# A planned mixer-and-MLP kernel on one core: a rank for every instruction in place of a rank for every kind, and another order of the first loads

## The chip, the cores and the metric

The kernel runs on one core of one Trainium2 chip. The time is the device time of that core in microseconds (us). A core has engines that run side by side, each strictly in its own order: PE (TensorE, matmuls; its weight loads are shown apart as PEld), DVE (VectorE), ACT (ScalarE), POOL (GpSimd), and SP (SyncE), which here only issues DMAs. The engines wait for each other through semaphores. PE writes to PSUM only, and ACT carries nearly every PSUM result back to SBUF ("evicts" it).

## The reference, cut to what matters

```python
x = A_q                                          # 2048 rows of 640, bf16
g = sigmoid((x * gate_w).sum(-1))
# branch A: a causal convolution of four taps on k, times v, then a convolution of length 2048 by FFT
k_shift = sum(k_pad[:, t:t+S] * shift_k[:, 3-t] for t in range(4))
kv = k_shift * v
y = irfft(rfft(kv, 2*S) * rfft(ssm_k, 2*S))[:S] + kv * ssm_D
a = q * y
# branch B: layer norm, w1, gelu, four column groups moved by +1, -1, +2, -2 rows, w2, residual, layer norm, w3, gelu, w4, residual
h = gelu(layernorm(x) @ w1);  x1 = x + shift_groups(h) @ w2
b = x1 + gelu(layernorm(x1) @ w3) @ w4
out = g * a + (1 - g) * b
```

## The kernel before

All data stays in one SBUF tensor ("arena"). The 2048 rows stand as 2 halves (c) of 128 partitions of 8 rows (r), so "row r" below means 2 x 128 rows of the matrix, and x comes in by pieces of some r of one c.

The program is written as a list of 924 nodes (`Prog.op`, `pe`, `dma`; class `Node`, lines 32 to 63), each with an engine, a planned cost, a tag such as `mm1` or `kv`, and what it depends on. `Prog._forward` (lines 200 to 347) then fixes the order of each engine: it keeps a planned clock of each engine and of the DMA link, and takes again and again the node that could start first; among nodes that could start at the same time the one with the higher `prio` goes first. `assign_waits` and `emit` turn the orders into instructions and semaphore waits. So a planned cost, the planned rate of the link (`RATE`) and the ranks change nothing in what is computed; they change in which order each engine does it, and each engine then keeps to that order even if the data of a later instruction is there first.

The tags, in the order of the work:

- `x`: loads of x, ten DMAs by `X_LOADS` (line 438). The pieces of row 0 go by ACT's queue, the others by SP's. `w1`, `shk`, `k`, `kh`, `v`, `w2`, `FM`, `ssm`, `D`, `gw`: the other loads on SP's queue (lines 707 to 736), all through `load` (line 692).
- `bn`, `st`, `ln`, `xn`: the first layer norm. Statistics by DVE (`bn`, lines 874 and 876; row 1 by ACT, `st`, line 666), the power -1/2 by POOL (line 854), normalized rows by DVE (`xn`, line 654).
- `xTp`, `xTe`: transposition by PE (line 913) and its eviction by ACT (line 680, as nearly all evictions).
- `mm1`, `gelu1`, `tail`: w1 (line 953), gelu, and small DMAs by POOL (line 993) that move column groups.
- `kv`, `kvb`: the four taps and v, on DVE (line 649, as all its tensor_tensor operations).
- `tap`, `ssmD`, `tT`, `tW`, `tR`: the filter `ssm_k` transposed, its first half by PE (line 809), its second by DMA.
- `seed2`, `mm2`, `x1`, `sq`: x is put into PSUM by ACT (line 1043), w2 is added by PE (line 1061), the sum is evicted with its row sums, and its squares are summed by ACT (line 666).
- `fwdh`, `Sh`, `fwdk`, `Sk`: forward transforms of filter and kv by PE (line 1164) and their evictions. `:0` and `:1` belong to the first half of the columns, `:2` and `:3` to the second.
- `bh`, `win`, `bk`, `pw`, `pwz`, `fold` (`unit`, line 1263): butterflies and pointwise products, all on DVE, for four units 0 to 3.
- `mm3`, `gelu3`, `seed4`, `mm4`, `B`: w3 (line 1115) and w4 (line 1133) with their gelu, seeds and evictions.
- `inv`, `invl`, `gy`, `fin`, `out`: inverse transforms (lines 1352 and 1327), gates and stores.
- `fill`: 96 matmuls on ones (line 744) that nobody reads; the planner puts them where PE would stand.

Slots are shared: the transforms of the second half are evicted into places that the units 0 and 1 read (`s3`, `s4`), so `fwdh:3` must wait until DVE's `pw:1` has read `s4`. PSUM is four pairs of banks, so PE can be a few jobs ahead of ACT's evictions.

Of the kernel before, what the change touches and what calls it, by code (L numbers as in the profile page):

```python
# [88 lines left out]
class Prog:  # L89
# [88 lines left out]

    PRIO = {}

    def schedule(self):
        for n in self.nodes:
            n.base = frozenset(n.deps)
        for j in self.jobs:
            own = set(j.nodes)
            j.ext = [d for v in j.nodes if not v.first for d in v.base if d not in own]
            if j.seeded:
                j.nodes[0].soft = [d for v in j.pes for d in v.base if d not in own]
        for n in self.nodes:
            for d in n.deps:  # L190
                d.users.append(n)
        for n in self.nodes:
            n.prio = self.PRIO.get(n.tag, 0.0)
        self._forward()

    RATE = 400e3
# [3 lines left out]
    def _forward(self):  # L200
# [14 lines left out]
        link = 0.0  # L215
# [5 lines left out]
        duty = carry = 0.0  # L221
        LAT = self.LAT
# [16 lines left out]
        while left:  # L239
# [42 lines left out]
            if n.array:  # L282
# [7 lines left out]
                if n.tag != "shk":  # L290
                    inside = min(cost, self.PHASE + (w + 1) * self.WINDOW - t)
                    duty += inside
                    carry += cost - inside
            free[e] = t + cost
# [7 lines left out]
            elif n.kind == "acc":  # L302
                alink = max(alink, t + 1.2) + n.bytes / 220e3
# [123 lines left out]
def _bf16_bits(a):  # L427
# [10 lines left out]
X_LOADS = ((0, 1), (1, 2), (2, 4), (4, 6), (6, 8))  # L438
# [16 lines left out]
PRIO = {  # L455
# [36 lines left out]
}  # L492
# [44 lines left out]
def bass_gated_mix__ssm_conv_h3__mixer_s_mlp__prompt_kernel(  # L537
# [168 lines left out]
    for a, b in X_LOADS:  # L706
        P.stage = a
        for c in range(2):
            load(XQ.get((a, c), "sp"), X[:, c, a:b, :], rows(A_q, c)[:, a:b, :], 163840 * (b - a), tag="x", land=1.4 if b < 3 else 2.2)
    P.stage = ""  # L710
    load("pool", V(oID, 256).bitcast(U16), cI.ap(), 65536, tag="ident", cost=0.6)
    load("sp", w1v, B_w1.rearrange("(c p) f -> p c f", p=128), 890000, tag="w1")
    load("sp", SHKROW, dram(A_shift_k, 0, [[2560, 1], [1, 2560]]), 5120, tag="shk")
    w1s, w1d = w1v.rearrange("p c (g f) -> p c g f", g=4)[:, :, :, 128:160], w1t.rearrange("p c (g f) -> p c g f", g=4)
    P.op("pool", lambda e, ps: e.tensor_copy(w1d, w1s), r=[w1s], w=[w1d], cost=1.2, tag="w1t")
# [101 lines left out]
    def add_d(h):  # L817
        t0row = TAP[0:1, h, 0, :]
        P.op("pool", lambda e, ps: e.tensor_tensor(t0row, t0row, DROW[h], ALU.add), r=[t0row, DROW[h]], w=[t0row],
             cost=2.0, tag="ssmD")  # L820
# [67 lines left out]
    def sum_group(rhos):  # L888
# [6 lines left out]
        ln_finish(VAR2, RS2, 2.3, rsl)  # L895
# [507 lines left out]
    P.PRIO = PRIO  # L1403
# [32 lines left out]
```

## Time and profile before

| what | value |
|---|---|
| median of 3 runs | 228.64 us (227.26 to 228.83) |
| profiled execution, its own time | 227.51 us |
| its span, first to last instruction | 225.7 us |
| DVE busy | 208.1 us |
| ACT busy | 174.8 us |
| PE weight loads (PEld) busy | 139.0 us |

The profiled execution's own time is 1.8 us above its span, and 1.1 us below the median. The profile's "PE busy" counts a matmul from its start to the end of its latency, so it overstates how full PE is. The chain of waits follows the work that ended last back through what released it. In the timeline, equal instructions in a row are merged: start, length, engine, line, shapes, count, and in brackets how long the engine had stood before and what ended that.

### The profile page before, as it was taken

The numbers are of one execution on the slowest core, as the hardware profiler recorded it, in microseconds if no ns is written. First come the engines' busy times: TensorE is split into PE (matmuls) and PEld (weight loads), VectorE is DVE, ScalarE is ACT, GpSimd is POOL, SyncE is SP. The second block draws the span as 40 slices with busy tenths as digits, with TensorE's granted clock in tenths as the row PEclk, the third lists the DMA queues.
The fourth block names the chain that finished last, engine by engine and source line by source line (L and its number), as shares of the span: only waits on it lengthen the run. The fifth ranks groups of instructions, "written<-read, shape, count | busy, mean of one in ns | idle before, by whom it ended". The sixth has DMA issues, their size and how long they took to land.

```text
span 225.7 us, 3992 instructions
## 1 busy us (share of the span) xinstructions
PE 217.8 (97%) x1575; PEld 139.0 (62%) x1587; DVE 208.1 (92%) x267; ACT 174.8 (77%) x292; POOL 42.6 (19%) x48
## 2 busy tenths in 40 slices
PE   6999999999999999999999999999999999999992
PEld 6695855557776664457754467754465566577771
DVE  4899999999999969999999999649999999999985
ACT  5889979879999999999785885594593465574392
POOL 1143654460004220203203200000010000332010
PEclk9999999999999999999999999999999999999999
DMA  6999997779823948061441680000077018488576
GB/s 166 392 401 402 334 348 251 151 143 243 281 96 84 310 85 341 7 116 33 87 86 30 108 130 0 3 0 0 0 132 219 0 35 200 58 174 110 126 135 215
DMA packets 36714, 34.05 MB, mean 151 GB/s; under 512 B 17508, under 2 KB 31719, under 8 KB 36568
## 3 DMA queue, kind: packets, MB, share of 16 engines
q1 hardware_dynamic: 31560, 23.97, 36.7%
q0 software_dynamic: 4848, 9.50, 19.2%
q10 hardware_dynamic: 288, 0.33, 0.5%
q8 instruction: 12, 0.20, 0.4%
q14 instruction: 6, 0.05, 0.1%
HBM read 21.47 MB, written 3.93 MB: 113 GB/s over the span
## 4 chain that ended last, share of the span: by engine, by line
PE 60%; DVE 24%; DMA 5%; issue 4%; ACT 4%; SPq 2%; DVEq 0%
PE PS L1133 23%; PE PS L1115 23%; DVE arena L649 20%; PE PS L1164 8%; PE PS L1352 6%; DMA arena<-in_A_q_dram 5%; ACT arena L680 3%; SPq L692 2%; DVE arena L874 2%; DVE arena L654 1%; PE PS L1061 1%; DVE arena L876 0%; ACT PS L1043 0%; DVE arena L1337 0%; DVEq L1406 0%
## 5 line engine op out<-in xcount | busy, mean ns | idle before, releaser
L649 DVE TENSOR_TENSOR arena<-arena 128x2560 bf16<-128x2560 bf16 (+5 forms) x175 | 185.9, 1120 | 10.4 <-ACT arena L680 8.9
L680 ACT ACTIVATE arena<-PS 128x640 bf16<-128x640 f32 (+6 forms) x142 | 104.9, 821 | 20.2 <-PE PS L1115 14.9
L1133 PE MATMUL PS<-arena 128*128 128x320 bf16 x384 | 54.0, 299 | 0.0
L1115 PE MATMUL PS<-arena 128*128 128x512 bf16 x232 | 51.4, 379 | 0.6 <-issue 0.2
L1133 PEld LDWEIGHTS PS<-arena 128*128 128x128 bf16 x384 | 37.4, 98 | 14.9 <-issue 0.3
L680 ACT ACTIVATE arena<-PS,arena 128x320 bf16<-128x320 f32 (+1 forms) x47 | 27.2, 616 | 22.5 <-PE PS L1133 20.2
L1115 PEld LDWEIGHTS PS<-arena 128*128 128x128 bf16 x240 | 23.3, 98 | 27.9 <-issue 0.3
L1164 PE MATMUL PS<-arena 128*128 128x320 bf16 x224 | 34.9, 300 | 0.7 <-DVE arena L649 0.4
L1164 PEld LDWEIGHTS PS<-arena 128*128 128x128 bf16 x224 | 20.6, 98 | 12.8 <-ACT arena L680 3.0
L666 ACT ACTIVATE arena<-arena 128x640 bf16<-128x640 bf16 (+2 forms) x34 | 25.9, 789 | 2.6 <-DVE arena L898 1.5
L1061 PE MATMUL PS<-arena 128*128 128x320 bf16 x160 | 23.4, 299 | 0.1
L953 PE MATMUL PS<-arena 128*128 128x512 bf16 (+1 forms) x121 | 22.8, 335 | 0.5 <-issue 0.2
L1043 ACT ACTIVATE PS<-arena 128x640 f32<-128x640 bf16 x32 | 22.6, 740 | 0.1
L854 POOL TENSOR_TENSOR arena<-arena 128x4 f32<-128x4 f32 (+1 forms) x9 | 12.9, 1441 | 39.3 <-DVE arena L654 33.2
L1061 PEld LDWEIGHTS PS<-arena 128*128 128x128 bf16 x160 | 15.2, 98 | 6.6 <-ACT PS L1043 0.7
L953 PEld LDWEIGHTS PS<-arena 128*128 128x128 bf16 x125 | 11.7, 98 | 8.5 <-DMA arena<-in_B_w_dram 0.3
L874 DVE BATCH_NORM_STATS2 arena<-arena 128x6 f32<-128x320 bf16 x28 | 12.1, 471 | 3.3 <-DMA arena<-in_A_q_dram 3.3
L688 POOL DMA_DIRECT2D arena<-arena x4 | 4.8, 1204 | 49.9 <-DVE arena L649 49.1
L1352 PE MATMUL PS<-arena 128*128 128x320 bf16 x96 | 13.7, 299 | 0.0
L1378 POOL DMA_DIRECT2D arena<-arena x4 | 5.1, 1275 | 42.5 <-DVE arena L649 40.4
L1352 PEld LDWEIGHTS PS<-arena 128*128 128x128 bf16 x96 | 9.3, 98 | 4.0 <-issue 0.2
L993 POOL DMA_DIRECT2D arena<-arena x18 | 10.1, 566 | 6.0 <-ACT arena L680 6.0
(42 smaller groups left out, 85.7 us busy)
## 6 DMA issues: line engine op xcount, KB each, us to landing
arena<-in_B_w_dram POOLq DMA_DIRECT2D x4, 960.0 KB, 7.9
arena<-in_A_k_dram SPq DMA_DIRECT2D x4, 640.0 KB, 13.7
arena<-in_A_v_dram SPq DMA_DIRECT2D x4, 640.0 KB, 14.8
arena<-arena POOLq DMA_DIRECT2D x4, 640.0 KB, 6.2
arena<-in_A_q_dram SPq DMA_DIRECT2D x4, 640.0 KB, 5.5
out_dram<-arena SPq DMA_DIRECT2D x15, 160.0 KB, 2.7
arena<-in_A_q_dram SPq DMA_DIRECT2D x6, 320.0 KB, 6.7
arena<-in_A_ssm_k_dram SPq DMA_DIRECT2D x3, 512.0 KB, 9.1
```

The costliest lines, as they stand in the source:

```text
L649: return dve(lambda e: e.tensor_tensor(o, a, b, op), [a, b], [o], c_tt(n), tag=tag, **kw)
L666: node = P.op("act", lambda e, ps: e.activation(o, i, func, **kw), r=r, w=[o], cost=c_act(n, naps, acc is not None, psum=False), tag=tag, ...
L680: node = P.op("act", lambda e, ps: e.activation(ov, inner(ps), func, **kw), r=r, w=[o], cost=c_act(n, len(r), acc is not None), job=job, t ...
L854: P.op("pool", lambda e, ps: e.tensor_tensor(r, v, hv, ALU.pow), r=[v, HALF], w=[r], cost=cost, tag="ln")
L874: dve(lambda e, o=o, x=x: e.bn_stats(o, x), [x], [o], 0.393, tag="bn", group=("bn", id(mv), rho, c))
L953: fns.append(lambda e, ps, b=b, c=c, lhsT=lhsT: e.matmul(bank(ps, b, 256 * n), lhsT, XT[:, c, r0:r0 + n, :], start=(c == 0), stop=(c == 4)))
L1043: P.seed(job, lambda e, ps: e.activation(two(ps, 320), x, ACTF.Copy), [X[:, c, rho, :]], c_act(640, psum=False), tag)
L1061: fns.append(lambda e, ps, hh=hh, ft=ft, lhsT=lhsT: e.matmul(bank(ps, hh, 320), lhsT, w2v[:, ft, 320 * hh:320 * hh + 320], start=False, st ...
L1115: fns.append(lambda e, ps, b=b, ft=ft, c=c, sc=sc: e.matmul(bank(ps, b, 512), w3h[ft // 6][:, c, 128 * (ft % 6):128 * (ft % 6) + 128], XT[ ...
L1133: fns.append(lambda e, ps, hh=hh, ft=ft, lhsT=lhsT: e.matmul(bank(ps, hh, 320), lhsT, w4h[ft // 6][:, ft % 6, 320 * hh:320 * hh + 320], st ...
L1164: fns.append(lambda e, ps, w=w, b=b, rhs=rhs, st=(first and n == 0), en=(n == len(ss) - 1): e.matmul(bank(ps, b, 320), w, rhs, start=st, s ...
L1352: fns.append(lambda e, ps, w=w, z=z, c=c, st=(n == 0), en=(n == len(terms) - 1): e.matmul(bank(ps, c, 320), w, z[:, c, :], start=st, stop=en))
```

## The change

Four things are changed, and nothing of what is computed.

1. The x loads: pieces of rows (0), (1), (2,3), (4,5), (6,7) become (0), (1,2), (3,4), (5,6), (7). The number of DMAs stays 10.
2. The ranks: before, all nodes of a tag shared one rank (`PRIO`, a dictionary by tag, of which `"fwdh:2": 219, "kvb:3": 215, ...` are examples); after, `RANK` is a list of 924 different numbers from 0 to 923, by the node's place in the program. SP's loads are all free to go from the start, so their ranks alone set their order.
3. The planner's model: rate of the link, landing times of x and w1, costs of some POOL operations, a rule by which a POOL operation and a long DVE operation slow each other, and accumulating DMAs that share the link.
4. The orders that come out of it on every engine.

```diff
-    PRIO = {}
+    PRIO = ()
...
-            n.prio = self.PRIO.get(n.tag, 0.0)
+            n.prio = self.PRIO[n.idx]
...
-    RATE = 400e3
+    RATE = 390e3
...
+            if n.kind == "c" and e == "pool":
+                if busy and free["dve"] > t + 0.2:
+                    cost *= 2.2
+                lock = t + cost
+            elif e == "dve":
+                busy = n.cost > 0.3 and n.tag[:2] != "bn"
+                if busy and lock > t + 0.1:
+                    cost += 0.48
+                    lock = 0.0
...
-                alink = max(alink, t + 1.2) + n.bytes / 220e3
+                alink = link = max(alink, link, t + 1.2) + n.bytes / 220e3
...
-X_LOADS = ((0, 1), (1, 2), (2, 4), (4, 6), (6, 8))
+X_LOADS = ((0, 1), (1, 3), (3, 5), (5, 7), (7, 8))
...
-PRIO = {
...
+RANK = [
+    920, 917, 905, 923, 915, 904, 888, 870, 898, 848, 853, 801, 812, 918, 877, 913, 779, 795, 738, 866, 753, 716, 721,
...
-            load(XQ.get((a, c), "sp"), X[:, c, a:b, :], rows(A_q, c)[:, a:b, :], 163840 * (b - a), tag="x", land=1.4 if b < 3 else 2.2)
+            load(XQ.get((a, c), "sp"), X[:, c, a:b, :], rows(A_q, c)[:, a:b, :], 163840 * (b - a), tag="x", land=1.5)
...
-    load("sp", w1v, B_w1.rearrange("(c p) f -> p c f", p=128), 890000, tag="w1")
+    load("sp", w1v, B_w1.rearrange("(c p) f -> p c f", p=128), 850000, tag="w1", land=1.7)
...
-    P.op("pool", lambda e, ps: e.tensor_copy(w1d, w1s), r=[w1s], w=[w1d], cost=1.2, tag="w1t")
+    P.op("pool", lambda e, ps: e.tensor_copy(w1d, w1s), r=[w1s], w=[w1d], cost=0.72, tag="w1t")
...
-             cost=2.0, tag="ssmD")
+             cost=0.8, tag="ssmD")
...
-        ln_finish(VAR2, RS2, 2.3, rsl)
+        ln_finish(VAR2, RS2, 1.0, rsl)
...
-    P.PRIO = PRIO
+    P.PRIO = RANK
```

In the printed line of `RANK`, places 3 and 4 are row 0's loads, 5 to 12 the other x pieces, 13 the identity, 14 `w1` (877), 15 `shk`, 19 a load of k (866). Sorted by rank, SP's queue begins: `gw`, `shk`, rows (1,2) of c=0, rows (3,4) of c=1, a `D`, rows (1,2) of c=1, one piece of `w2`, `w1`, rows (3,4) of c=0, one load of k, both pieces of rows (5,6), `FM:0`, `ssm:1`, `ssm:2`, both pieces of row 7, `k:0`. Before, it was: row 1, `gw`, rows (2,3), `shk`, `ssm:0`, rows (4,5), `w1`, `ssm:1`, rows (6,7), `FM`, loads of k.

The orders of the other engines can be read roughly from the list in the same way, by sorting an engine's nodes by rank. It is rough, since the planner takes a node with a lower rank first where it could start earlier. Read so, these are the larger moves on PE:

| place in PE's order | before | by rank after |
|---|---|---|
| `mm2` jobs (of 16) ahead of the first `fwdk` | 14 | 16 |
| `fwdh:0`, `fwdh:1` jobs (of 16) ahead of the first `fwdk` | 16 | 14 |
| `gate` jobs (of 4) ahead of the first `fwdk` | 4 | 3 |
| `fwdk` jobs ahead of the first `mm3` | 20 | 16 |
| first `fwdh:3` | after `mm3:0`, `mm4:0`, `mm3:1` and part of `mm4:1` | after `mm3:0`, `mm4:0` and 7 jobs of `mm3:1`, `mm3:2` |
| first `inv:0` | after `mm4:2` has begun | before `mm4:1` |

ACT's and DVE's orders follow: the `Sk:2` evictions move behind the first `gelu3`, and on DVE the statistics of row 7 come last of the first layer norm.

More of the change, by code (lines that the diff above doesn't have):

```diff
@@ L221, in _forward @@
         duty = carry = 0.0
+        busy, lock = False, 0.0
         LAT = self.LAT
@@ L454 @@
 SEED4 = (0, 1, 2, 3, 4, 5, 6, 7)
-PRIO = {
[36 rows of a table removed]
-}
+RANK = [
[40 rows of a table added]
+]
 def _freq(kap):
```

75 rows, old and new, of tables (PRIO, RANK) are left out of this document.

## The prediction

> **What bounds the kernel now.** I read the page first, then the chain of waits in order of time, then busy time by stretches, then single rows of the timeline.
>
> ```profile
> span 225.7 us, 3992 instructions
> PE 60%; DVE 24%; DMA 5%; issue 4%; ACT 4%; SPq 2%; DVEq 0%
> ```
>
> The chain belongs to DVE early and to PE late. Its pieces in order of time show where it changes hands:
>
> ```profile
> 70.98 1.50 DVE arena L649
> 72.48 0.05 issue
> 72.53 0.73 PE PS L1164 x4
> 73.28 2.49 ACT arena L680 x4
> ...
> 86.00 10.74 PE PS L1115 x49
> 96.74 0.05 issue
> 96.79 2.10 PE PS L1115 x9
> ...
> 206.34 6.52 PE PS L1133 x48
> ```
>
> At 72.5 us the last `kvb` of DVE ends and the first `fwdk` starts. At 86.00 the first `mm3` starts. From the chain come the prices of PE: six `mm3` jobs of 10 matmuls take 86.00 to 98.89, 12.89/60 = 0.215 us a matmul (two of the 60 have no record); a matmul of 320 columns costs 6.52/48 = 0.136 us.
>
> How full the engines are in three stretches, of all instructions, and then of line 1061 (`mm2`) and line 1164 (`fwd`) alone:
>
> ```profile
> 0.00:72.53 72.53, 69.71 (x641) 48.67 (x646) 67.31 (x104) 64.76 (x116) 22.82 (x34) 1.00 0.80 252
> 72.53:86.00 13.47, 13.22 (x95) 8.45 (x96) 11.51 (x20) 13.39 (x27) 3.74 (x3) 1.00 0.74 203
> 86.00:221.56 135.56, 134.90 (x840) 81.87 (x846) 127.67 (x141) 96.30 (x152) 16.06 (x11) 1.00 0.43 90
> 72.53:86.00 13.47, 3.06 (x20) 1.88 (x20) 1.00 0.74 203
> 72.53:86.00 13.47, 10.65 (x72) 6.37 (x72) 1.00 0.74 203
> 86.00:225.70 139.70, 15.33 (x96) 8.92 (x96) 1.00 0.43 93
> ```
>
> The columns are PE, PEld, DVE, ACT, POOL (busy us and count), the granted clock, the DMA share and GB/s. Up to 72.5 DVE has 67.3 us of work and can't be bought off: its waits are listed below. From 72.5 to 86 ACT is full (13.39 of 13.47). PE there has 20 + 72 matmuls x 0.136 = 12.5 us of work, so it loses 1.0. After 86.00 PE has 240 `mm3` matmuls x 0.215 = 51.6 and 384 + 96 + 96 + 32 matmuls of 320 columns (`mm4`, `fwd`, `inv`, `invl`; counts in these rows) x 0.136 = 82.7 us, together 134.3 of 135.56: it loses 1.3 us in all. So after 72.5 us a reordering can win at most about 2.3 us, unless more of PE's work gets ahead of 72.5.
>
> ```profile
> L1115 PEld LDWEIGHTS PS<-arena 128*128 128x128 bf16 x240 | 23.3, 98 | 27.9 <-issue 0.3
> L1133 PE MATMUL PS<-arena 128*128 128x320 bf16 x384 | 54.0, 299 | 0.0
> L1352 PE MATMUL PS<-arena 128*128 128x320 bf16 x96 | 13.7, 299 | 0.0
> ```
>
> ```profile
> 217.05 4.51 PE L1327 MATMUL PS<-arena 128*128 128x320 bf16 x32
> ```
>
> **The change, part by part.** *The loads.* These rows carry them: DVE's three waits for x and its first `kv`, PE's wait for w1, the size of w1, and the rate of the link in the loading stage.
>
> ```profile
> 3.76 0.89 DVE L874 BATCH_NORM_STATS2 arena<-arena 128x6 f32<-128x320 bf16 x2 [2.05 <-DMA arena<-in_A_q_dram]
> 6.88 0.89 DVE L874 BATCH_NORM_STATS2 arena<-arena 128x6 f32<-128x320 bf16 x2 [0.79 <-DMA arena<-in_A_q_dram]
> 16.45 1.31 DVE L874 BATCH_NORM_STATS2 arena<-arena 128x6 f32<-128x320 bf16 x3 [0.48 <-DMA arena<-in_A_q_dram]
> 23.28 2.82 DVE L649 TENSOR_TENSOR arena<-arena 128x5120 bf16<-128x5120 bf16 x1
> 11.73 1.42 PE L744 MATMUL PS<-arena 128*128 128x128 bf16 x21
> 13.29 0.77 PEld L953 LDWEIGHTS PS<-arena 128*128 128x128 bf16 x8 [0.31 <-DMA arena<-in_B_w_dram]
> arena<-in_B_w_dram SPq DMA_DIRECT2D x1, 800.0 KB, 8.5
> 15.20 0.78 DVE L654 TENSOR_SCALAR arena<-arena 128x640 bf16<-128x640 bf16 x2
> 5.64:16.45 10.81, 10.65 (x141) 8.39 (x139) 9.48 (x32) 9.15 (x16) 3.24 (x4) 1.00 1.03 394
> ```
>
> Pieces land in the order of the queue at 394 GB/s. Ahead of w1 stand, before, 2.5 MB (rows 0 to 5 and `ssm:0`), after 1.5 MB (rows 0 to 2, half of rows 3 and 4, a piece of `w2`): 1.0 MB/394 GB/s = 2.6 us, so w1 lands near 10.7 instead of 13.3. PE has in that place only fills (1.42 us) and a wait of 0.31. So the earlier w1 can give PE 0 to 1.7 us; I take 1.1, the amount that the next paragraph needs. The other side: row 7 becomes the last x piece, behind w1, a k, `FM:0`, `ssm:1`, `ssm:2`. Before, 4.5 MB ended with the last x; after 5.8 MB: 1.3 MB more, 3.4 us. The wait at 16.45 was for one of the last two pieces of 0.33 MB, the other is 0.8 us behind it: 17.3, after 20.7. DVE's work between 3.76 and 23.28 is 19.5 less the waits 0.79 and 0.48, 18.25 us. With no wait at all it reaches `kv` at 22.0, 1.3 earlier. But by the ranks four statistics of row 7 (0.89/2 each), three normalizations (0.78/2) and a few small operations stand between row 7 and `kv`, some 3.2 us; the first of its two pieces of 0.16 MB lands at 20.3, which gives 23.5, 0.2 later than before. The upper end: the same sum, started at w1's 13.3, would have had the last x of before at 16.3 (1.2 MB further), and it was there 1.0 later; so +1.2. Between -1.3 and +1.2 I take 0, which is near the +0.2 that the rows give.
>
> *PE's and ACT's orders around 72.5.* Two `mm2` jobs (20 matmuls, 2.7 us) go ahead of 72.5; behind it go two `fwdh` jobs (at most 8 matmuls, 1.1 us) and one `gate` job of 0.64:
>
> ```profile
> 61.74 0.64 PE L1010 MATMUL PS<-arena 128*128 128x1 bf16 x20
> 78.97 8.46 ACT L680 ACTIVATE arena<-PS 128x640 bf16<-128x640 f32 x14
> 34.01 9.24 ACT L680 ACTIVATE arena<-PS 128x1024 bf16<-128x1024 f32 x15 [1.30 <-PE PS L953]
> 43.93 1.62 ACT L680 ACTIVATE arena<-PS 128x1024 bf16<-128x1024 f32 x2 [0.69 <-PE PS L953]
> 46.70 1.03 ACT L680 ACTIVATE arena<-PS 128x1024 bf16<-128x1024 f32 x1 [1.14 <-PE PS L953]
> ```
>
> Net 1.0 us of PE's work moves ahead of 72.5, worth 1.0 if PE finds that time before (the 1.1 of w1) and ACT the evictions: one seed, two sums and their read-outs, about 2 us at these prices, less a `Sh`. ACT waited for PE for 1.30 + 0.69 + 1.14 = 3.1 us between 34 and 47, so it has the room. If not, this term is 0. In the stage after 72.5 ACT evicts a `Sk` in 8.46/14 = 0.604 us while PE makes one in 4 x 0.136 = 0.544 or less. 16 `Sk`, a `Sh` and a `zz` are about 10.6 us of ACT against 56 x 0.136 + 1.1 + 0.64 = 9.4 of PE: PE loses 1.2, where it lost 1.0 before, since no `mm2` is left to fill in. That is -0.2 of the gain. The four `fwdk:2` jobs that go behind `mm3:0` cost nothing: between two `mm3` jobs (2 x 2.15 us) ACT has two gelus and two squares and room for one more eviction.
>
> *The rest.* After 86.00 the same jobs come in another order, and only the 1.3 us of lost time can be won. The evenly mixed transforms should save the stretch where eight evictions in a row held PE up; I take 0.3 (ends: all 1.3 won, or a new wait, the second rival). DVE waits for ACT for 8.9 us there:
>
> ```profile
> DVE arena L649 <- ACT arena L680: 8.9, 4, 3.4
> ```
>
> The earlier transforms shorten these waits, but PE is full meanwhile, so that is worth nothing by itself. The lowered costs of POOL's operations only steer the planner. The tail after PE's last matmul, two small DVE operations and a store, stays.
>
> [...] PE's first fills ran at 4.41/48 = 92 ns each and those just before w1 at 1.42/21 = 68 ns, with a granted clock of 1.00 in the rows above:
>
> ```profile
> 1.75 4.41 PE L744 MATMUL PS<-arena 128*128 128x128 bf16 x48 [1.75 <-DVE arena L702]
> ```
>
> [...]
>
> **The sum.** 0 (DVE's front) - 1.0 (work ahead of 72.5) + 0.2 (ACT-bound stage) - 0.3 = -1.1 us. The profiled execution took 227.51, 1.1 less than the median 228.64, so the sum gives 226.4 there and 227.5 as a median: 0.5% faster.
>
> **The rivals.** *Faster: PE is fed earlier everywhere.* w1's 1.7 us are used in full, DVE's two waits go (1.3), and the 1.3 lost after 86.00 goes too. Since DVE's 72.5 moves by 1.3, the end gains 1.3 + 1.0 + 1.3 = 3.6 us: 225.0. For it speaks that w1 truly stops PE at 13.29; against it the late row 7.
>
> *Slower: PE and ACT stand at slot `s4`.* By the ranks `fwdh:3` comes after 13 `mm3` jobs, 4 `mm4` and 35 small matmuls: 130 x 0.215 + 131 x 0.136 = 45.8 us after the first `mm3`. That `mm3` starts at about 72.5 + 0.7 + 10.6, less two jobs that PE is ahead (1.2): 82.6. So PE is there at 128.4. Before, it came at 133.87, after DVE's fifth `pw:1` in this row was done:
>
> ```profile
> 133.87 0.71 PE L1164 MATMUL PS<-arena 128*128 128x320 bf16 x4
> 124.59 16.09 DVE L649 TENSOR_TENSOR arena<-arena 128x2560 bf16<-128x2560 bf16 x13
> ```
>
> Five operations of 1.40 after 124.59 end at 131.6. With three jobs (1.6 us) ahead in PSUM, PE would stand 131.6 - 130.0 = 1.6 us if DVE is no earlier. Behind `Sh:3` on ACT wait the gelus of `mm3`, so PE has nothing else. DVE should be a little earlier, since its `Sk:0` come sooner. This rival decides the sign once the stand passes 1.1 us and the 1% once it passes 3.4; with 4.0, when DVE is some 2.4 later than before, the time is 228.64 - 1.1 + 4.0 = 231.5.
>
> *Nothing changes*: the extra work ahead of 72.5 doesn't find room, and the terms cancel: 228.6.
>
> **How the numbers follow.** About 1% is what a measurement of this kernel can tell from no change. The forecast case gets 0.36; its own range, by the ends of DVE's front, is 226.2 to 228.7, and with the other ends a quarter of it (0.09) falls below 226.35, which is 1% under 228.64. No effect (228.6) gets 0.11. The fast rival gets 0.25: w1's move rests on a row, and an order made for each instruction can win what I don't see. The slow rival gets 0.28 beyond 230.9: an order of 924 places has many spots like `s4`. So faster 0.25 + 0.09 = 0.34, same 0.27 + 0.11 = 0.38, slower 0.28. The range for 8 in 10 goes from 224.2, a little below the fast rival, to 231.5, the slow one; I leave out some 0.08 below and 0.11 above.
>
> **What would show it.** w1 right: the first row of line 953 starts near 11 to 12 instead of 13.29. DVE's front: `kv` starts between 22.0 and 24.5. Work ahead of 72.5: no row of line 1061 after the first `fwdk`. ACT-bound stage: the first `mm3` near 82.6. Slot `s4`: a row of line 1164 or 680 with a wait for line 649 near 130. The forecast is wrong if PE is no longer full after the first `mm3`, or if the first `fwdk` moves by more than 1.3 us.

## The result and the profile after

The changed kernel takes 225.93 us in the median of 15 runs (225.46 to 227.16), the kernel before, run beside it, 227.70 us (227.14 to 229.54). The ratio is 0.9902, with a 95% interval of 0.9881 to 0.9924: about 1% faster. The profiled execution took 225.55 us with a span of 223.5, where before it was 227.51 with 225.7. Forecast were 1.1 us less; measured are 1.8 by the medians and 2.2 by the spans.

The page of the changed kernel, its span and the shares of the chain that ended last. Lines of the code lie 14 further down than before, so `mm3` is L1129, `mm4` L1147, `fwd` L1178, `mm2` L1075, `mm1` L967:

```profile
span 223.5 us, 3945 instructions
PE 76%; ACT 18%; DVE 2%; DMA 2%; issue 1%; SPq 0%; ACTq 0%
```

The chain's pieces in order of time (start, length, what):

```profile
40.77 2.17 PE PS L967 x10
42.97 2.21 ACT arena L694 x3
...
72.45 9.74 ACT arena L694 x18
82.54 4.26 PE PS L1129 x19
...
127.72 3.62 PE PS L1178 x26
...
217.01 3.98 DVE arena L663 x15
```

Before, DVE's `kv` and `kvb` carried the chain up to 72.5 us. Now it is PE up to 42.9, then ACT without a break up to 82.2, then PE to the end. DVE's own work still ends at the same time: the last `kvb` at 72.66 instead of 72.47. From 43 to 72 us PE, DVE and ACT are now all full (28.9, 28.5 and 28.8 of 29.0 us; before 28.9, 28.7 and 27.2), and the chain of this page runs along ACT.

Busy time by stretches, of all instructions, then of `mm2` alone (PE, PEld, DVE, ACT, POOL with counts; granted clock, DMA share, GB/s):

```profile
0.00:72.46 72.46, 70.27 (x621) 48.51 (x625) 66.73 (x100) 66.03 (x118) 22.82 (x34) 1.00 0.76 251
72.46:82.54 10.08, 9.20 (x80) 6.14 (x82) 9.05 (x19) 10.08 (x20) 1.83 (x3) 1.00 0.86 250
82.54:219.80 137.26, 136.86 (x856) 83.38 (x862) 131.45 (x145) 97.92 (x156) 16.48 (x12) 1.00 0.42 91
0.00:72.46 72.46, 22.58 (x160) 15.36 (x160) 1.00 0.76 251
72.46:223.50 151.04, 0.00 (x0) 0.00 (x0) 1.00 0.46 105
```

All 160 `mm2` matmuls stand ahead of 72.46; before, 20 of them came behind the first `fwdk`. ACT is full in the second stretch. Single rows of the timeline (start, length, engine, line, count, and the time stood before):

```profile
9.79 0.72 POOL L729 COPY arena<-arena 128x640 bf16<-128x640 bf16 x1 [2.74 <-DMA arena<-in_B_w_dram]
11.61 1.80 PE L967 MATMUL PS<-arena 128*128 128x256 bf16 x15
22.60 1.44 DVE L663 TENSOR_TENSOR arena<-arena 128x2560 bf16<-128x2560 bf16 x1
72.81 5.31 PE L1178 MATMUL PS<-arena 128*128 128x320 bf16 x36 [0.56 <-DVE arena L906]
82.54 1.67 PE L1129 MATMUL PS<-arena 128*128 128x512 bf16 x7 [0.46 <-ACT arena L694]
```

w1 is there at 9.7 (POOL's copy of a part of it starts at 9.79), the first `mm1` runs at 11.6, the first `kv` at 22.60 (23.28 before), the first `fwdk` at 72.81 (72.53), the first `mm3` at 82.54 (86.00). In the waits, the line that stood for 8.9 us before is now:

```profile
DVE arena L663 <- ACT arena L694: 3.5, 5, 1.6
```

The difference of the spans can be worked out from these starts. The first `fwdk` is 0.28 later. From there to the first `mm3` it took 13.47 and takes 9.73: 20 `mm2` matmuls (2.72) have gone ahead and 16 of `fwdk:2` (2.18) behind, one `fwdh` (0.54) and one `gate` (0.64) have come in. From the first `mm3` to PE's end it took 135.56 and takes 137.26, 1.70 more: the 2.18 of `fwdk:2`, less 0.5 that PE no longer loses. That is 0.28 - 3.74 + 1.70 = -1.76 at PE's end (221.56 to 219.80), and the tail behind it is 0.46 shorter: -2.2.

### The profile page after: what moved, and what is told of

It is laid out like the page before. It is cut to its first block, busy times and chain, and to the rows that moved or that the text cites. A ratio compares the mean times of both kernels' runs of the same rounds, so it can differ in the third digit from the quotient of the medians.

```text
span 223.5 us, 3945 instructions
## 1 busy us (share of the span) xinstructions
PE 216.3 (97%) x1557; PEld 138.0 (62%) x1569; DVE 208.7 (93%) x267; ACT 174.6 (78%) x292; POOL 41.1 (18%) x48
## 4 chain that ended last, share of the span: by engine, by line
PE 76%; ACT 18%; DVE 2%; DMA 2%; issue 1%; SPq 0%; ACTq 0%
PE PS L1147 23%; PE PS L1129 23%; ACT arena L694 12%; PE PS L1178 9%; PE PS L967 8%; PE PS L1366 6%; ACT PS L1057 5%; PE PS L927 2%; ACT arena L680 2%; DVE arena L663 2%; DMA arena<-in_A_q_dram 2%; PE PS L823 1%; PE PS L769 1%; PE PS L758 1%; PE PS L780 0%
## 5 line engine op out<-in xcount | busy, mean ns | idle before, releaser
L694 ACT ACTIVATE arena<-PS 128x640 bf16<-128x640 f32 (+8 forms) x142 | 104.2, 812 | 18.9 <-PE PS L1129 14.7
L1147 PE MATMUL PS<-arena 128*128 128x320 bf16 x384 | 53.3, 299 | 0.0
L1129 PE MATMUL PS<-arena 128*128 128x512 bf16 x232 | 52.2, 379 | 0.8 <-ACT arena L694 0.5
L1147 PEld LDWEIGHTS PS<-arena 128*128 128x128 bf16 x384 | 37.4, 98 | 15.0 <-issue 0.3
L694 ACT ACTIVATE arena<-PS,arena 128x320 bf16<-128x320 f32 (+1 forms) x47 | 27.7, 626 | 24.2 <-PE PS L1147 22.2
L1129 PEld LDWEIGHTS PS<-arena 128*128 128x128 bf16 x240 | 23.3, 98 | 27.4 <-issue 0.5
L1178 PE MATMUL PS<-arena 128*128 128x320 bf16 x224 | 34.4, 300 | 0.7 <-DVE arena L906 0.6
L1178 PEld LDWEIGHTS PS<-arena 128*128 128x128 bf16 x224 | 20.8, 98 | 12.8 <-ACT arena L694 2.8
L680 ACT ACTIVATE arena<-arena 128x640 bf16<-128x640 bf16 (+2 forms) x34 | 25.8, 787 | 0.8 <-DMA arena<-in_A_q_dram 0.4
L967 PE MATMUL PS<-arena 128*128 128x512 bf16 (+1 forms) x121 | 22.9, 335 | 0.2
L1075 PE MATMUL PS<-arena 128*128 128x320 bf16 x160 | 22.6, 299 | 0.0
L868 POOL TENSOR_TENSOR arena<-arena 128x4 f32<-128x4 f32 (+1 forms) x9 | 14.0, 1553 | 30.7 <-DVE arena L668 30.4
L1075 PEld LDWEIGHTS PS<-arena 128*128 128x128 bf16 x160 | 15.4, 98 | 6.7 <-ACT PS L1057 0.6
L967 PEld LDWEIGHTS PS<-arena 128*128 128x128 bf16 x125 | 11.8, 98 | 8.2 <-ACT arena L694 0.5
L1366 PE MATMUL PS<-arena 128*128 128x320 bf16 x96 | 14.3, 299 | 0.0
```

The source lines that it names most:

```text
L680: node = P.op("act", lambda e, ps: e.activation(o, i, func, **kw), r=r, w=[o], cost=c_act(n, naps, acc is not None, psum=False), tag=tag, ...
L694: node = P.op("act", lambda e, ps: e.activation(ov, inner(ps), func, **kw), r=r, w=[o], cost=c_act(n, len(r), acc is not None), job=job, t ...
L868: P.op("pool", lambda e, ps: e.tensor_tensor(r, v, hv, ALU.pow), r=[v, HALF], w=[r], cost=cost, tag="ln")
L967: fns.append(lambda e, ps, b=b, c=c, lhsT=lhsT: e.matmul(bank(ps, b, 256 * n), lhsT, XT[:, c, r0:r0 + n, :], start=(c == 0), stop=(c == 4)))
L1075: fns.append(lambda e, ps, hh=hh, ft=ft, lhsT=lhsT: e.matmul(bank(ps, hh, 320), lhsT, w2v[:, ft, 320 * hh:320 * hh + 320], start=False, st ...
L1129: fns.append(lambda e, ps, b=b, ft=ft, c=c, sc=sc: e.matmul(bank(ps, b, 512), w3h[ft // 6][:, c, 128 * (ft % 6):128 * (ft % 6) + 128], XT[ ...
```

## The experiments

"Held orders" below means that every engine keeps the order of the kernel named but for the nodes that the diff moves. In `relink` and `SEAT` lists a number is a node's place in the program; the triple names an engine, the nodes moved, and the node behind which they come. In "re-planned" runs only ranks change, and the planner makes new orders from them. Inserted lines shift line numbers by up to 60.

**Late w1.** The first experiment puts w1 back behind rows 5 and 6, with the orders of the changed kernel held (27 is the piece of `w2`, 14 is w1, 9 a piece of rows 5 and 6).

```diff
     P.schedule()
+    P.relink([("sp", [27, 14], 9)])
```

> The changed kernel with only SP's queue altered: w1 and the piece of w2 ahead of it go behind both pieces of rows (5,6); every order of the computing engines is that of the changed kernel. Theory 1 (the gain comes from PE's early start: the chain after the change is PE from 6.2 us to 42.9 and ACT from there to 82.2, so what PE loses before mm1 is lost at the end): w1 lands 1.48 MB later, 3.7 us, near 13.4; the first row of line 967 moves from 11.8 to about 13.4, the first mm3 from 82.5 to about 84, the time grows by 1.2 to 1.6 us, ratio to before 0.995 to 0.997. Theory 2 (the gain comes from the order of mm2, fwdk and mm3, and the loads are hidden anyway): x rows 3 to 6 land earlier, the first mm3 stays within 0.4 of 82.5, ratio 0.989 to 0.992.

Measured: ratio 1.0158 (1.0126 to 1.0190), span 230.6; both theories missed it. w1 landed at 15.3 and the first `kv` came at 29.40, 6.8 later than in the changed kernel; everything behind is shifted by 6.6 to 7.2 us. Windows of this run, the columns as above:

```profile
12.00:14.00 2.00, 0.91 (x5) 0.17 (x3) 1.23 (x5) 1.59 (x3) 0.00 (x0) 1.00 1.08 385
14.00:16.00 2.00, 0.00 (x0) 0.00 (x0) 0.00 (x0) 0.00 (x0) 0.65 (x1) 0.72 1.03 402
16.00:18.00 2.00, 1.88 (x9) 1.35 (x10) 1.24 (x5) 0.38 (x1) 0.72 (x2) 0.50 1.03 394
18.00:20.00 2.00, 2.00 (x15) 1.61 (x13) 2.00 (x8) 0.46 (x1) 1.63 (x2) 0.50 1.03 399
20.00:22.00 2.00, 2.00 (x12) 1.12 (x10) 1.92 (x8) 1.54 (x3) 0.00 (x0) 0.57 1.06 392
```

and its rows in that place:

```profile
15.35 0.71 POOL L756 COPY arena<-arena 128x640 bf16<-128x640 bf16 x1 [7.89 <-DMA arena<-in_B_w_dram]
16.03 0.69 POOL L895 TENSOR_TENSOR arena<-arena 128x2 f32<-128x2 f32 x1
16.12 3.38 PE L994 MATMUL PS<-arena 128*128 128x256 bf16 x15 [3.21 <-POOL arena L756]
16.76 0.80 DVE L695 TENSOR_SCALAR arena<-arena 128x640 bf16<-128x640 bf16 x2 [3.53 <-POOL arena L895]
```

Between 14 and 16 us nothing runs but POOL's copy. In POOL's new order that copy stands ahead of the power -1/2 of row 1 (`ln:1`), which has nothing to do with w1. DVE's normalization of row 1 waits for `ln:1`, and PE for w1. PE stands for 3.21 us, from 12.9 to 16.1, and the granted clock is 0.50 from about 14.9, two microseconds into the stand, until about 21.7: 15 `mm1` matmuls take 3.38 us where they took 1.80. So a load that is 5.6 us late costs 7 us at the end, with these orders, where the term in the prediction for its being earlier was 1.1.

**Early w1 without the new orders.** The kernel before, its orders held, with w1 ahead of `ssm:0` and rows (4,5):

```diff
     P.schedule()
+    P.relink([("sp", [14], 15)])
```

> The kernel before with only SP's queue altered: w1 goes ahead of ssm:0 and rows (4,5), so that it lands about 2.6 us earlier, near 10.7; all other orders stay. If an early w1 is worth something by itself: first mm1 near 11.5 instead of 13.3 and ratio 0.993 to 0.996. If it needs the orders made for it: ssm:0 now lands 2 us later and holds up the first tap on PE, ACT still evicts that tap ahead of the first gelu, so mm1 starts between 12.3 and 13.3 and the ratio is 0.998 to 1.003.

Measured: ratio 1.0040 (1.0012 to 1.0067), span 226.4. w1 landed at 10.0 instead of 13.3, `ssm:0` at 11.3 instead of 9.4. PE's rows (L836 is `tap`, L771 `fill`, L980 `mm1`):

```profile
11.32 1.19 PE L836 MATMUL PS<-arena 128*128 128x128 bf16 x16
12.34 1.34 PE L771 MATMUL PS<-arena 128*128 128x128 bf16 x21
13.51 1.25 PE L980 MATMUL PS<-arena 128*128 128x256 bf16 x10
```

The orders have `tap:0`, which needs `ssm:0`, and fills in front of the first `mm1`, so it runs at 13.51, no earlier than before (13.29), and the first `kv` comes at 24.12 (23.28). By itself the early load brings nothing; `mm1` and the ratio even came out a little beyond the ends of the second expectation (13.3 and 1.003).

**Late w1 with orders that allow for it.** As the first, but what needs w1 is queued later as well: POOL's copy behind `ln:2`, five `mm1` jobs and their evictions behind the transposes of rows 1 to 3. For this the planner takes from each engine only the next node of a given list, `SEAT`, the changed kernel's orders with these moves:

```diff
                 for n in ready[e]:
+                    if n.idx != SEAT[e][len(order[e])]:
+                        continue
...
+# sp: 27, 14 behind 9; pe: 293, 289, 291, 299, 297, 295 behind 233
+# act: 294, 290, 292, 300, 298, 296 behind 234; pool: 16, 302 behind 230
```

> w1 and the piece of w2 stand behind rows 5 and 6 as in the run with the late w1, but what needs w1 is queued later as well: POOL's copy of w1 behind the statistics of rows 1 and 2, the first five mm1 jobs on TensorE and their evictions on ScalarE behind the transposes of rows 1 to 3. Theory (the late w1 cost 7 us because in-order queues held other work behind it and TensorE, left without work for 3.2 us, ran at half its clock afterwards): the stand and the half clock go, first kv 22.5 to 23.5, span 223.5 to 225.5, ratio 0.990 to 0.999. Rival (w1's own lateness carries the cost through mm1, gelu and mm2): first kv is back but the span stays at 227 or more, ratio 1.005 or more.

Measured: ratio 1.0122 (1.0084 to 1.0161), first `kv` at 28.49, span 229.9. The theory's numbers didn't come. Of the rival's, span and ratio came, but the first `kv` isn't back. The rows show why:

```profile
19.82 1.28 DVE L948 BATCH_NORM_STATS2 arena<-arena 128x6 f32<-128x320 bf16 x3 [1.30 <-DMA arena<-in_A_q_dram]
26.48 0.80 DVE L728 TENSOR_SCALAR arena<-arena 128x640 bf16<-128x640 bf16 x2 [5.38 <-POOL arena L928]
...
24.31 1.08 POOL L1067 DMA_DIRECT2D arena<-arena  x2 [2.74 <-ACT arena L754]
25.40 1.04 POOL L928 TENSOR_TENSOR arena<-arena 128x4 f32<-128x4 f32 x1
```

POOL's next row power (`ln:4`, L928) stands behind `tail` DMAs, which wait for the first `gelu1`, which waits for w1. DVE stands 5.38 us for it. So a second place of the same kind had been left in POOL's order. PE stands for 2.69 us in front of the transposes of 16.69, and its clock is 0.50 from about 18.0 to 21.5 here too. How much would remain with all of them mended was not tried. What both runs show is that the new orders need w1 early at several places at once.

**Row 7 earlier.** Row 7 ahead of `FM:0`, `ssm:1`, `ssm:2`, orders held:

```diff
+    P.relink([("sp", [12, 11], 9)])
```

> The changed kernel with only SP's queue altered: both pieces of row 7 go ahead of FM:0, ssm:1 and ssm:2, so that they land near 15.8 instead of 19.8. If DVE's front sets the first fwdk and the end: DVE's wait of 0.42 us for row 7 goes, kv and the first fwdk come 0.4 us earlier, ratio 0.988 to 0.989. If PE's chain of the first 43 us and ACT's after it set it: no gain, and taps that come 0.9 us later may cost PE up to 0.5, ratio 0.990 to 0.993.

Measured: ratio 0.9934 (0.9899 to 0.9968), first `kv` at 23.02. No gain: the late row 7 costs nothing that the ratio shows. It landed at 16.4 instead of 19.8 and DVE no longer waits for it; but in this execution w1 and the pieces behind it landed later (w1 at 11.0), and DVE stood 1.12 us for one of them at 11.87.

**A power of POOL's ahead of `kv`.** In the changed kernel `ln:6` on POOL runs beside DVE's `kv`, and DVE stands 0.93 us for it. Here DVE finishes the statistics before the first `kv`:

```diff
+    P.relink([("dve", [269, 272, 273], 267)])
```

> The changed kernel with one thing altered on DVE: the last two aggregations and ln:6 go ahead of the two normalizations of row 5, so that POOL gets its power for rows 6 and 7 while DVE runs normalizations and not while it runs kv with two inputs of SBUF. In the changed kernel that POOL operation takes 3.54 us at 24.21, and DVE stands 0.93 us for it at 27.8. Expected in any case: POOL's operation takes about 1.0 to 1.5 us and the stand of 0.93 goes. If DVE sets the first fwdk and the end: kvb ends 0.7 to 0.9 us earlier and the time falls by 0.4 to 0.9 us, ratio 0.986 to 0.988. If ACT, full from 43 us to the first mm3, sets it: first mm3 within 0.3 of 82.5, ratio 0.989 to 0.991.

The operation in the changed kernel, and in this run:

```profile
24.21 3.54 POOL L868 TENSOR_TENSOR arena<-arena 128x4 f32<-128x4 f32 x1 [2.96 <-DVE arena L668]
```

```profile
22.82 1.16 POOL L895 TENSOR_TENSOR arena<-arena 128x4 f32<-128x4 f32 x1 [1.51 <-DVE arena L695]
```

3.54 becomes 1.16 and DVE's stand goes, but the ratio is 0.9904 (0.9870 to 0.9937), the same as the changed kernel's. The last `kvb` ends 0.2 earlier (72.44), the first `mm3` 0.1 (82.42): ACT, full up to there, sets it.

**The last two `mm2` jobs behind the first `fwdk`, re-planned.** Their seeds, matmuls and read-outs are seated behind the first `Sk:0` in the list of ranks:

```diff
-    P.PRIO = RANK
+    seat = sorted(range(len(RANK)), key=lambda i: -RANK[i])
+    # [452] behind 614, [448] behind 612, [453] behind 452, [449] behind 448, [454, 450] behind 619
...
+    for k, i in enumerate(seat):
+        P.PRIO[i] = len(seat) - k
```

> The changed kernel with the last two mm2 jobs of PE (their seeds, sums and squares with them) given lower ranks than the fwdk jobs, so that PE does them between the fwdk and the mm3 jobs, as 20 matmuls of 0.136 behind 72.5 us. One gate job and one fwdh job move ahead in their place. Theory (PE's work still to do at 72.5 sets the end): 2.7 us more, 0.9 less for the gate and fwdh job, some 0.3 regained where ACT held up PE: the time grows by 1.2 to 1.8 us, ratio 0.995 to 0.998. Rival (ACT's load up to the first mm3 sets it, and the order of these jobs on PE is indifferent): ratio 0.989 to 0.992.

Measured: ratio 1.0143 (1.0105 to 1.0180), span 229.0. The start of `gelu3` moves by only 1.0 (85.66), but the first `B:0` by 5.9.

**The four `fwdk:2` ahead of the first `mm3`, re-planned.** The same with nodes 742, 743, 750, 751, 746, 747, 754, 755 behind 616.

> The changed kernel with four fwdk:2 jobs and their Sk:2 evictions ahead of the first mm3 again, as before the change; small reorderings of ACT's later work follow from the planner. Theory (only the work left counts, and moving these four behind mm3 was free): the first mm3 starts 2.2 to 2.5 us later, near 84.9, but the time grows by only 0 to 0.4 us, ratio 0.990 to 0.992. Rival (the earlier start of mm3 is the gain itself): the time grows by 2 us or more, ratio 0.998 to 1.000.

Measured: ratio 1.0183 (1.0141 to 1.0225), span 229.3. `gelu3` comes 2.5 later (87.22), PE's end 5.9. Most of the other 3.4 us are lost at `mm4`, where PE (first row) waits for a seed that ACT (second row) makes only at 107.89, behind normalizations (L680) of rows that are needed later:

```profile
108.65 3.43 PE L1147 MATMUL PS<-arena 128*128 128x320 bf16 x24 [2.47 <-ACT PS L1057]
107.89 0.71 ACT L1057 ACTIVATE PS<-arena 128x640 f32<-128x640 bf16 x1
```

A change of eight ranks had changed the order of everything behind. These two runs therefore say little of the moved jobs, and both moves were made again with held orders.

**The four `fwdk:2`, orders held.**

```diff
+# pe: 742, 750, 746, 754 behind 616; act: 743, 751, 747, 755 behind 629
```

> The changed kernel with every engine's order held as it is, but for the four fwdk:2 jobs and their Sk:2, which stand ahead of the first mm3 as in the kernel before. Theory (the prediction's: these four cost nothing where they are, and bring nothing): first mm3 2.2 to 2.5 later, span within 0.6 of 223.5, ratio 0.990 to 0.994. Rival (their place buys the gain, as the re-planned run's 1.018 would have it): span 225.5 to 229, ratio 1.000 or more.

```profile
84.64 7.71 PE L1189 MATMUL PS<-arena 128*128 128x512 bf16 x35 [0.18 <-issue]
```

Measured: the first `mm3` at 84.64, 2.1 later, PE's end 0.5 later (220.27), span 223.9, ratio 0.9924 (0.9898 to 0.9950). That overlaps with the changed kernel's interval. Some three fifths of the 3.46 by which `mm3` starts earlier were work pushed behind it, and brought at most half a microsecond.

**The last two `mm2` jobs, orders held.**

```diff
+# pe: 453, 449 behind 630; act: 454, 450 behind 631
```

> The changed kernel with every engine's order held as it is, but for the last two mm2 jobs and their two read-outs, which stand behind the third fwdk job. Theory (work ahead of 72.5 is worth what TensorE can't hide later): 20 matmuls x 0.136 = 2.7 us move behind, TensorE lost 0.9 in that stage, so the end is 1.8 later: span 225 to 226, ratio 0.997 to 1.002; first mm3 1.2 later by the two evictions. Rival (TensorE's holes in the stage bound by ScalarE take both jobs up, or no difference can be seen): span within 0.5 of 223.5, ratio 0.990 to 0.993. Second rival (what the re-planned run showed belongs to these jobs): span near 229.

Measured: ratio 1.0133 (1.0076 to 1.0190), which is 3 us over the kernel before and 5 over the changed one. In the profiled execution (233.68 us, span 231.6, mean clock 0.975), which is not among the five that the ratio rests on, the clock also fell in the front, and the last `kvb` came 1.6 later. Around the moved jobs its windows and PE's rows (L1238 is `fwd`, L1135 `mm2`) are:

```profile
70.00:72.00 2.00, 0.97 (x24) 0.77 (x22) 2.00 (x4) 2.00 (x6) 0.62 (x1) 1.00 0.00 0
72.00:74.00 2.00, 0.72 (x4) 0.31 (x4) 1.90 (x2) 2.00 (x8) 1.10 (x2) 0.85 0.46 58
74.00:76.00 2.00, 1.63 (x7) 0.94 (x8) 0.50 (x4) 0.72 (x2) 1.03 (x1) 0.50 0.97 382
76.00:78.00 2.00, 1.21 (x6) 0.39 (x5) 0.00 (x0) 1.04 (x2) 0.00 (x0) 0.50 1.03 369
78.00:80.00 2.00, 2.00 (x9) 1.19 (x8) 0.00 (x0) 0.70 (x1) 0.00 (x0) 0.50 0.49 174
```

```profile
72.41 0.72 PE L1238 MATMUL PS<-arena 128*128 128x320 bf16 x4 [1.45 <-ACT arena L754]
74.37 2.29 PE L1238 MATMUL PS<-arena 128*128 128x320 bf16 x8 [1.24 <-ACT arena L754]
78.50 3.73 PE L1135 MATMUL PS<-arena 128*128 128x320 bf16 x20
```

Without the two jobs PE has nothing to do at 71 to 72 us, stands for 1.45 and 1.24 us, and from about 73.4 to 80.2 its clock is halved. The two jobs (L1135) take 3.73 us, where the row of the last two took 2.88 in the changed kernel, and ACT, whose order holds their read-outs in front of the next `Sk`, is busy for only 2.46 of the 6 us from 74 to 80, although it is what bounds this stage.

The five runs of the ratio show how much of this is the clock. Three had a mean clock of 0.983 to 0.985 and took 232.57 to 233.02 us; two had 1.000 and took 229.61 and 229.69. By an estimate, 0.016 of 231 us is what some 7 us at half the clock leave, about as long as the stretch from 73.4 to 80.2; where it lay in those runs no trace shows. So some 3 of the 5 us go with the clock. With the clock whole, the moved jobs cost 1 us over the kernel before (228.69 beside these runs) and, by the ratio 0.9902, some 3 over the changed one. That is more than the theory's 1.8, and the second rival's span of 229 lies between the two kinds of run. What ACT's order adds to the 2.7 us of the two jobs was not separated.

**The two late `mm2` jobs of the kernel before put ahead, its orders held.**

```diff
+# pe: 420, 424 behind 416; act: 423, 421, 425 behind 417
```

> The kernel before with every engine's order held as it is, but for the two mm2 jobs that ran behind the first fwdk: they and their evictions stand directly behind the one before them. Theory (they can go ahead only where TensorE has room there, and the room came from the early w1): TensorE stands idle for only 0.5 us between 45 and 72.5, so 2.7 us more there push other work back: first fwdk 0.5 to 2 later, span 225.2 to 226.5, ratio 0.998 to 1.004. Rival (the order alone brings the gain): span 223.5 to 224.5, ratio 0.990 to 0.995.

```profile
77.14 2.54 PE L1224 MATMUL PS<-arena 128*128 128x320 bf16 x16
```

Measured: ratio 1.0042 (1.0017 to 1.0067), 229.31 us. The order of these jobs alone brings nothing in the kernel before, as the theory had it. The theory's place and span were too low: the first `fwdk` comes 4.6 later (the row above) in the profiled execution, and the span is 228.4 there and 226.8 to 227.3 in the runs with a mean clock of 1.00. In the profiled one the clock was halved from 10.6 to 14.0 and the last `kvb` came 1.5 later, so not all of the 4.6 is the jobs'. The early w1 and these two jobs together were not run in the kernel before; that it is the early w1 that makes the room for them is therefore argued, not shown.

**The tail.** The changed kernel ends with another order of the last inverse transforms; here they come again in program order:

```diff
+    # 888 to 923 behind 870, in program order
```

> The changed kernel with the split inverse jobs at the end in pairs again and 7b last: 6a 6b 4a 4b 5a 5b 7a 7b, where the changed kernel makes 7b early and 7a last. Up to the inverse of the second half nothing moves. Theory (0.4 us of the gain lie behind PE's last matmul, because one store instead of two is issued after the last DVE operation; after PE's end the span goes on for 3.7 us now and 4.1 before): the span behind PE's last matmul grows by 0.3 to 0.5 us, ratio 0.991 to 0.993. Rival (the tail is a matter of chance in the store's landing): no growth, ratio 0.989 to 0.991.

Measured: ratio 0.9927 (0.9900 to 0.9953), span 223.6. No difference that can be told from the changed kernel. From PE's end to the end of the span it took 3.9 us here, 3.7 in the changed kernel, but 4.0 in the runs on row 7 and on `ln:6`, which keep its tail and ran on the same chip as this one. So the order of the last jobs is not shown to matter. On the two other chips of the experiments the tail does go with the kernel: 3.67 to 3.69 in all six runs that keep the changed one's (late w1 twice, `mm2` and `fwdk:2` twice each), 4.01 and 4.26 in the two of the kernel before. What makes it shorter stays open.

**Ranks by tag on the new loads.** The new pieces, load order and model, but for all other nodes the old ranks by tag:

```diff
-    P.PRIO = RANK
+    P.PRIO = [1000 + RANK[n.idx] if n in loads else TAGS.get(n.tag, 0.0) for n in P.nodes]
```

> The changed kernel, loads and planner model included, but the computing engines' ranks are taken by tag from the dictionary of before; SP's loads keep their ranks of after. It asks what the list of ranks by itself carries. Theory (the old ranks were found for the old loads and costs, and orders must be made for them): PE, DVE and ACT lose their fit, among others a mm1 and its gelu of row 0 come late and hold up the tail moves and mm2; the time grows by 3 to 15 us over before, ratio 1.01 to 1.06. Rival (the model and the loads carry the gain, the ranks only break ties): ratio 0.985 to 0.998.

Measured: ratio 1.2629 (1.2569 to 1.2689). Of its waits, and of its windows the one from 90 to 130:

```profile
DVE arena L702 <- ACT arena L733: 53.1, 9, 22.1
PE PS L1217 <- ACT arena L733: 28.4, 6, 22.5
```

```profile
90.00:130.00 40.00, 18.07 (x130) 12.06 (x128) 39.97 (x51) 31.80 (x71) 9.75 (x6) 0.77 0.25 45
```

PE is busy for 18 of 40 us there and stands for 22.5 us, up to 131.0, for an eviction of ACT's, while DVE is full. DVE's own longest stand for an eviction, 22.1 us, ends at 244.7. The old ranks belonged to the old loads and model; with others the planner falls into an order that leaves PE empty, and the mean clock drops to 0.92. It shows how much hangs on ranks and model fitting each other, not what the ranks by node are worth.

## Why the prediction was nearly right

**Right in sign and nearly in size.** The sum was -1.1 us, measured are -1.8. The forecast median of 227.5 and the measured 225.93 lie further apart, since the 228.64 that it starts from was the median of three runs, and that of fifteen is 227.70; 225.93 is below 226.2, the lower end of the forecast case's own range. By its steps:

- *w1 and the first `mm1`*: forecast near 10.7 and 11 to 12; 9.7 and 11.6 (9.8 to 11.0 and 11.4 to 12.0 in the seven experiments on the changed kernel that keep w1's place in the queue and PE's first order). The early load without the orders (1.0040) and the orders without the early load (1.0158) are both slower than before, so each needs the other. That the load gives PE the time for other work ahead of 72.5 is not shown by that: the 7 us of the late w1 come by POOL's order and the clock. The prediction put a price of at most 1.7 us on the load. It didn't look at what stands behind w1 in POOL's order, and there a late w1 costs 7 us.
- *DVE's front*: taken as 0; the first `kv` comes 0.7 earlier, the first `fwdk` 0.28 later. Row 7 being last costs nothing that the ratio shows.
- *Work ahead of 72.5*: forecast net 1.0 (2.7 less two `fwdh` and a `gate`); 1.5, since only one `fwdh` came behind. The jobs did find room. Of all terms this is the largest; put back, the two jobs cost some 3 us at full clock.
- *The stage bound by ACT*: -0.2 was forecast, as a loss of 1.2 against 1.0; PE loses 0.93 there (9.73 less 60 matmuls of 0.136 and a `gate`). First `mm3` forecast at 82.6, measured 82.54. That this agrees to 0.1 is luck: the stage starts 0.3 later than the 72.5 of the forecast and takes 0.4 less than its 10.1.
- *Four `fwdk:2` cost nothing*: borne out with held orders (0.9924; 0.4 us in the spans).
- *The dense part*: 0.3 of the 1.3 lost were to be won; 0.5 are. (The 8.9 us of DVE's waits, put behind 86.00 in the prediction, hold one of 1.9 that ended at 82.1; no term rests on it.)
- *The tail*: forecast as unchanged; 0.46 shorter in the profiled executions, its cause open.

**The slow rival** at slot `s4` didn't come. `fwdh:3` runs in the piece of the chain from 127.72, with no wait. PE got there near 128, as forecast. DVE's fifth `pw:1` ended at 130.0, 1.6 earlier than the row of before had it, and I had priced the slot as if the whole of it came free at once: the three `Sh:3` evicted first, at 129.26 to 131.2, go to parts of it that the `pw:1` operations ended by 127.2 had read, and the next one comes at 134.51, behind the last `pw:1` (132.9). **The fast rival** needed all three gains in full; DVE still waits for x, 1.2 us in three waits behind the first one (1.3 in two before).

**The clock.** The forecast's sum has no term for PE's granted clock. For the profiled execution of the changed kernel that was right: it is 1.00 in the three stretches above, up to PE's end. But one step away the clock decides the size. With w1 late it was 0.50 for some 6.8 us, and with two `mm2` jobs fewer ahead of 72.5 the same happened there. In the first trace the clock fell 2.0 us into a stand of 3.21; in the second it fell at about 73.4, where PE had stood 1.45 us, worked for 0.72 and stood again, for 1.24.

In runs without a trace the kernel before does lose its clock: of 56 of its runs beside the experiments 28 had a mean clock of 0.988 to 0.992 and took 228.8 us in the median, 28 had 0.995 or more and took 227.6. Of the fifteen of the changed kernel two had 0.989 (226.90 and 227.16 us). So a part of the 1.8 us between the medians may be that the clock falls less often; no experiment separates it.

## What to carry to other kernels

A load order and the engines' orders made for it are one thing: half of such a change can be slower than none, so neither half's worth can be read from the whole. When a load is moved, look on every queue, the small engines' too, for what stands behind its first consumer. And when an order is tested, hold all other orders fixed, since a planner that may re-plan changes far more than what was asked: the same four jobs gave 1.0183 re-planned and 0.9924 held.

## What the runs showed of the hardware

- In two runs the granted clock halved without a long stand. The run of the kernel before with two `mm2` jobs ahead, windows of the front:

```profile
8.00:10.00 2.00, 2.00 (x20) 1.13 (x18) 2.00 (x8) 0.87 (x3) 0.00 (x0) 1.00 1.03 399
10.00:11.00 1.00, 1.00 (x6) 0.27 (x5) 1.00 (x5) 1.00 (x2) 0.00 (x0) 0.80 1.05 387
11.00:12.00 1.00, 1.00 (x11) 1.00 (x11) 1.00 (x6) 0.79 (x2) 0.69 (x2) 0.50 1.09 389
...
13.00:14.00 1.00, 1.00 (x12) 1.00 (x11) 1.00 (x2) 0.53 (x2) 0.71 (x1) 0.50 1.02 396
14.00:16.00 2.00, 2.00 (x30) 1.90 (x29) 0.94 (x4) 1.76 (x1) 0.00 (x0) 1.00 1.04 401
```

  By the granted clock it lasted some 3.4 us, from 10.6 to 14.0, and as long, from 12.0 to 15.4, in the run of the two held `mm2` jobs. There PE had stood 0.43 us, here not at all by the rows; in both the clock fell near the end of eight matmuls of a single row (`shk`, 1*128), which is at 10.96 here and at 11.91 there. In the changed kernel and the kernel before the same eight end at 11.55 and 10.24, and in the profiled execution the clock stays at 1.00. No run varied these matmuls alone, so what brought the clock down is not shown. Nor does PE's busy time tell it: here PE was busy for all of 8 to 10, and in the re-planned run of the `mm2` jobs for only 3.00 of the 5 us from 100, with the clock at 1.00 there and in the 5 us behind:

```profile
100.00:105.00 5.00, 3.00 (x21) 1.68 (x20) 4.93 (x6) 5.00 (x8) 0.00 (x0) 1.00 0.41 80
105.00:110.00 5.00, 4.77 (x31) 2.96 (x31) 4.93 (x8) 5.00 (x9) 1.14 (x1) 1.00 0.58 115
```

- The power -1/2 of four numbers a partition took POOL 3.54 us in the changed kernel, where it began at 24.21, 0.18 behind the start of a `kv` operation of DVE's that ran from 24.03 to 26.85. It took 1.16 in the run on `ln:6`, where it began at 22.82, 0.53 ahead of DVE's first `kv` operation there (23.35), and 1.12 in the kernel before, at 22.43, 0.85 ahead of the `kv` of 23.28. In these three it was long only where `kv` had begun first; what held it is not shown. Here it cost nothing at the end: without it the ratio is 0.9904.
